# Pooled attention and a softplus feed-forward layer: the transposes of q and of the probabilities in the steady part, by the DMA crossbar instead of TensorE

## The chip, the core and the metric

The kernel runs on one core of a Trainium2 chip. The metric is the device time of one execution in microseconds (us). The engines are named as the profile names them: PE (TensorE; PEld is its weight load), DVE (VectorE), ACT (ScalarE), POOL (GpSimd) and SP (SyncE), whose queue (SPq) issues all transfers of this kernel.

## What is computed

Attention with keys and values that are averaged in eights, then a feed-forward layer with a softplus, all in float32:

```python
# q, k, v: (8, 8, 576, 64)    w_in: (512, 2048)    w_out: (2048, 512)
k_p = k.reshape(B, H, Sp, 8, D).mean(axis=3)            # Sp = 72
v_p = v.reshape(B, H, Sp, 8, D).mean(axis=3)
scores = matmul(q, k_p^T) / sqrt(D)
attn = exp(scores - max) ; attn = attn / (sum(attn) + 1e-9)
x = (attn @ v_p) as rows of 4608 tokens x 512
g = softplus(x @ w_in)
out = g @ w_out                                         # (4608, 512)
```

## The kernel before

The 4608 tokens are worked in 18 chunks of 256 (two tiles of 128). A chunk `c` has its attention, which gives x transposed (512 x 256, split into a high part and a rest, `x` and its low half), and then eight pairs `u` = 0 to 7 of feed-forward blocks. For each pair PE makes the first products `h` (24 matmuls, L687), ACT and DVE turn them into softplus values and their sums (`g`, `gh`, `gl`, `sf`, `so`: L695 to L768), and PE makes the second products `m` (21 matmuls, L839) one pair later. So PE's row in the steady part reads h of pair u, m of pair u-1, h of pair u+1, m of pair u, and so on. In the text below h(7) is the first product of the last pair of a chunk, m(6) the second product of pair 6. ACT's and DVE's work on a pair must be done by the time PE comes to its m.

The attention of the next chunk is fitted in between. In the steady part (`steady_attention` and `probabilities`, chunks 4 to 17) its steps are: SP loads q (256 KB a tile, L363); PE transposes q of both tiles (`qTp<-ident,q`, 8 transposes of 128 x 128, L394) and ACT copies them to `qT` (L401); PE makes the scores into two PSUM banks and half of a third (`sc`, and `m` with kT as operand; L522); DVE takes minima (`mn`, L544) and writes the differences to `E` (L560); ACT takes the exponential of `E` (L355), after the third step of pair 2 (`EXP, third = 2, {}`); DVE takes sums, reciprocals and the probabilities (`pm`, L454, 128 x 512 a tile; `pe`, L570, the last few columns); PE transposes `pm` of both tiles (`ptp`, 8 transposes, L475) and ACT copies them to `pT` (L482); PE transposes `pe` (`ltp`, L575), ACT and DVE split that (`lt__`, L581, L585); PE makes the products with the values (`avp`, L601 and L608); ACT and DVE write x (L615, L618). The first half of h(0) of the next chunk reads this x.

The order on ACT, DVE, PE and SP is not the order of the code. Each step is entered with `op(engine, cost, fn, after, slots)`: a cost in us, the steps it comes after, and the buffers (`Slot`) that it takes. `Order.run` lays all steps of the steady part out in one list by these costs, and the kernel is issued in that order (`tc.manual_schedule`). Each engine then works its own list in order. A step may be laid out only when its slots are free in this plan. What matters below are these kinds:

```python
kinds = {"h": other[:2], "acc": other[2:4], "bank": other[4:], "ld": LD, "q": "a", "pT": "a", "qT": Q, "lt_": "a",
         "pe": "a", "mn": "ab", "sm": "ab", "E": "a", "kp": "a", "vp": "a", "S": "ab", "x": "b",
```

`other` has six PSUM banks, so there are two of kind `bank`. Scores take both until DVE has read them; `qTp` takes two, `ptp`, `ltp` and kT one each, `avp` both. There is one `E`, one `q`, one `pT`, and two `qT`. The weights `wi` of a pair (2 x 512 KB) are loaded again for every chunk and pair (L867) into one of two places, when PE has done the first products of the pair two before.

Of the kernel before, what the change touches and what calls it, by code (L numbers as in the profile page):

```python
# [9 lines left out]
F32 = mybir.dt.float32  # L10
F32R = mybir.dt.float32r
I32 = mybir.dt.int32
AF = mybir.ActivationFunctionType
ALU = mybir.AluOpType
AX = mybir.AxisListType
# [15 lines left out]
class Order:  # L31
# [14 lines left out]
    def op(self, engine, cost, fn, after=(), slots=(), lag=None, rest=0, first=0, table=None, run=None, home=None):  # L46
        o = Op(engine, cost, fn, after, slots, self.HOP if lag is None else lag, len(self.ops))
        o.rest, o.first, o.table, o.run, o.home = rest, first + self.first, table, run, home
        for x in o.after:
            x.followers.append(o)  # L50
        for x in slots:
            x.users.append(o)
        self.ops.append(o)
        return o
# [54 lines left out]
def pooled_attention_softplus_ffn(  # L109
# [9 lines left out]
    nc = tc.nc  # L119
    nc.scalar.preload_act_table_set("exp_and_others")  # L120
    B, H, S, D = q.shape
    NTOK, DM = out.shape
    DFF = w_in.shape[1]
    P = 128
    POOL = 8
    SP = S // POOL
    KM = 64
    KL = SP - KM
    T = 2
    CT = T * P  # L130
    HP = H // 2
# [14 lines left out]
    one = ctx.enter_context(tc.tile_pool(name="one", bufs=1))  # L146
# [95 lines left out]

    wi32, wo32 = w_in.bitcast(I32), w_out.bitcast(I32)
    NS = 3
# [18 lines left out]
    def k_scaled(b, ps):  # L263

        nc.scalar.activation(out=kT[b % 2], in_=ps[:, 0:HP * SP].rearrange("p (m y) -> p m y", m=HP),
                             func=AF.Copy, scale=SCALE)

    def v_scaled(b, vp):
        nc.scalar.activation(out=vs[b % 2], in_=vp, func=AF.Copy, scale=1.0 / POOL)

# [65 lines left out]
    qt_, x_, e_, pt_, last_ = {}, {}, {}, {}, {}  # L336
# [17 lines left out]
    def exponential(E):  # L354
        nc.scalar.activation(out=E, in_=E, func=AF.Exp, scale=-1.0)  # L355

# [27 lines left out]
    class Tile:  # L384
# [49 lines left out]
        def exp_sum(self, j, ps, tag):  # L434
            if j == 0:
                self.sm = small.tile([P, H], F32, tag="sm" + tag, name="sm")
            for m in range(HP):
                h = 4 * (m // 2) + 2 * j + m % 2
                nc.scalar.activation(out=e_[self.c][:, self.t, h], in_=self.view(ps)[:, m],  # L439
                                     func=AF.Exp, scale=-1.0, bias=self.mn[:, j, m:m + 1],  # L440
                                     accum_out=self.sm[:, h:h + 1])
# [60 lines left out]

    order_dep = mybir.DependencyInfo(mybir.DependencyClass.Sync, mybir.DependencyReason.DATA)
    between_out = small.tile([P, 8], F32, tag="between", name="between")
# [367 lines left out]
    op = todo.op  # L875
    ACT, DVE, PE, SYNC = (nc.scalar.engine, nc.vector.engine, nc.tensor.engine, nc.sync.engine)
    todo.begin, todo.table = {SYNC: 0.8}, "exp"

    def bank(s, name):
        if s.tile is None:  # L880
            s.tile = psum.tile([P, 512], F32, tag=s.name, name=name)
        return s.tile
# [3 lines left out]
    def act(n):  # L886
        return 0.14 + 0.00094 * n

    def dve1(n):
        return 0.14 + 0.00054 * n  # L890
# [7 lines left out]
    def weights(f):  # L898
# [5 lines left out]
        def load(i):  # L904
            def fn():
# [4 lines left out]
                else:  # L910
                    st = x["raw", i] = one.tile([P, 4 * 2 * P], I32, tag=stages[i].name, name="wst")
                if i:
# [24 lines left out]
        def bits(k):  # L937
# [4 lines left out]
            else:  # L942
                g = x["g", k] = one.tile([P, 1, 4 * P], I32, tag=gslot[k].name, name="wg")
                up = x["raw", k].unsqueeze(1).rearrange("p x (n w) -> p x n w", w=2)[:, :, :, 1]
# [160 lines left out]
    qT_done, score_done, av_done, k_ready, v_ready, made = {}, {}, {}, {}, {}, {}  # L1105
# [173 lines left out]
    o = op(DVE, 0.3, lambda: x_w.append(ones()), first=2000)  # L1279
# [49 lines left out]
    op = todo.op  # L1329
    EXP, third = 2, {}  # L1330
    HURRY, EARLY = 60, 100
    MM = 0.1142
    x_slot, x_done = {N1: taken[-1]}, {N1: []}
    for x in (qT_done, score_done, av_done, k_ready, v_ready):
        x.clear()
# [4 lines left out]
    def steady_attention(c):  # L1340
        s_q, s_E, s_lt = Slot("q"), Slot("E"), Slot("lt_")
        tiles = [Tile(c, t) for t in range(T)]

        def load():
            load_q(c)
        o_q = op(SYNC, 3.0, load, qT_done.get(c - 1, ()), [s_q], lag=2.4)
        subs = []
        qT_done[c], score_done[c], av_done[c], x_done[c] = [], [], [], []
        sp, s_mn, x_q = spans(c * CT, (c + 1) * CT), Slot("mn"), []
        s_qT, s_qb = [Slot("qT") for _ in tiles], [Slot("bank") for _ in tiles]  # L1350

        def transposes():
            for x, s in zip(tiles, s_qb):
                x.qT(bank(s, "qTp"))
        o = op(PE, 0.89, transposes, [o_q, *av_done.get(c - 1, ())], [s_q, *s_qb], first=EARLY, home="m")
        qT_done[c].append(o)
        for x, s, n in zip(tiles, s_qb, s_qT):
            x_q.append(op(ACT, act(512), lambda x=x, s=s, n=n: x.qT_out(s.tile, n.name), [o], [s, n]))
        old = c - 2 if c - 2 >= NF else None
        ss = [Slot("bank"), Slot("bank"), Slot("acc") if old is None else banks_of[old][3]]  # L1360

        def third_bank():
            return bank(ss[2], "sc") if old is None else ms[old]["rest"]
        p = op(PE, 1.4, lambda: pair_scores(
            c, tiles, [*(bank(s, "sc") for s in ss[:2]), (third_bank(), old is None)]),
               [*x_q, *parts_of(sp, k_ready), m_begun.get(old)], [*s_qT, *ss], first=EARLY, home="m")
        score_done[c].append(p)
        for j in (2, 0, 1):
            ps = lambda j=j: third_bank() if j == 2 else ss[j].tile
            o = op(DVE, 0.3 if j == 2 else 0.68,  # L1370
                   lambda j=j, ps=ps: pair_least(c, j, ps(), s_mn.name), [p], [ss[j], s_mn],
                   first=HURRY if j == 2 else 0)
            for part in range(1 if j == 2 else 3):
                subs.append(op(DVE, 0.3 if j == 2 else (0.46, 0.3, 0.22)[part],
                               lambda j=j, ps=ps, part=part: pair_less(c, j, part, ps()), [o],
                               [ss[j], s_mn, s_E], first=HURRY if j == 2 else 0))
        return lambda where: probabilities(c, tiles, s_E, s_lt, subs, where)

    def probabilities(c, tiles, s_E, s_lt, subs, where):

        s_pT, lows, s_pe, es = Slot("pT"), [], Slot("pe"), []
        ex = op(ACT, 1.2 + TABLE, lambda: exponential(e_[c]), [*subs, where], [s_E])
        op(ACT, TABLE, lambda: None, [ex], first=5000)
        for x in tiles:
            s_sm, s_pm = Slot("sm"), Slot("G")
            o = op(DVE, 0.76, lambda x=x, n=s_sm: x.sum(n.name), [ex], [s_E, s_sm])
            o = op(DVE, 0.38, x.reciprocal, [o], [s_sm])
            m = op(DVE, 0.7, lambda x=x, s=s_pm: x.main(s.name), [o], [s_E, s_sm, s_pm])
            es.append(op(DVE, 0.23, lambda x=x, s=s_pe: pair_ends(c, x, s.name), [o], [s_E, s_sm, s_pe]))
            s = Slot("bank")  # L1390
            o = op(PE, 0.45, lambda x=x, s=s: x.PT(bank(s, "ptp")), [m], [s, s_pm], first=EARLY, home="h")
            lows.append(op(ACT, act(512), lambda x=x, s=s: x.PT_out(s.tile), [o], [s, s_pT]))
        s_l = Slot("bank")
        p = op(PE, 0.23, lambda: pair_last(c, bank(s_l, "ltp")), es, [s_l, s_pe], first=EARLY, home="m")
        for a in range(2):
            h = op(ACT, act(256), lambda a=a: pair_high(c, a, s_l.tile, a), [p], [s_l, s_lt])
            lows.append(op(DVE, dve2(256), lambda a=a: pair_low_ends(c, a, s_l.tile), [h], [s_l, s_lt]))
        for a in range(2):
            lows.append(op(ACT, act(256), lambda a=a: pair_high(c, a, s_l.tile, 2), [p], [s_l, s_lt]))

        def values(after=()):
            sp = spans(c * CT, (c + 1) * CT)
            ss = [Slot("bank"), Slot("bank")]
            o = op(PE, 1.7 if len(sp) == 1 else 2.15,
                   lambda: av_products(c, [bank(s, "avp") for s in ss]),
                   [*lows, *parts_of(sp, v_ready), *after], [*ss, s_lt, s_pT], first=EARLY, home="h")
            av_done[c].append(o)
            return o, ss
        o, ss = values()
        s_x = x_slot[c] = Slot("x")  # L1410
        for r, s in enumerate(ss):
            o = op(ACT, act(512), lambda r=r, s=s: av_high(c, r, s.tile, s_x.name), [o], [s, s_x])
            x_done[c].append(op(DVE, dve2(512), lambda r=r, s=s: av_low(c, r, s.tile), [o], [s, s_x]))
# [171 lines left out]
```

## Time and profile before

| | |
|---|---|
| median of 3 runs | 880.64 us (880.38 to 880.72) |
| span of the profiled execution | 880.5 us |
| PE busy | 869.2 us |
| DVE busy | 644.7 us |
| ACT busy | 418.7 us |
| DMA, HBM traffic over the span | 216 GB/s |

The span reaches from the first to the last instruction of the profiled execution; 0.1 us more lies between it and the median. The steady part repeats every 46.4 us (first products of pair 1 of two neighbouring chunks start at 701.29 and 747.69). In the profile's rows, "x8" counts instructions, the second number of a timeline row is the length of the merged group, and in brackets stands how long the engine sat idle before it and who ended that. A matmul's row includes its way through the array, so neighbouring PE rows overlap: what one costs PE is the distance between starts.

### The profile page before, as it was taken

The numbers are of one execution on the slowest core, as the hardware profiler recorded it, in microseconds if no ns is written. First come the engines' busy times: TensorE is split into PE (matmuls) and PEld (weight loads), VectorE is DVE, ScalarE is ACT, GpSimd is POOL, SyncE is SP. The second block draws the span as 40 slices with busy tenths as digits, with TensorE's granted clock in tenths as the row PEclk, the third lists the DMA queues.
The fourth block names the chain that finished last, engine by engine and source line by source line (L and its number), as shares of the span: only waits on it lengthen the run. The fifth ranks groups of instructions, "written<-read, shape, count | busy, mean of one in ns | idle before, by whom it ended". The sixth has DMA issues, their size and how long they took to land.

```text
span 880.5 us, 21346 instructions
## 1 busy us (share of the span) xinstructions
PE 869.2 (99%) x8706; PEld 845.9 (96%) x8706; DVE 644.7 (73%) x1601; ACT 418.7 (48%) x852; POOL 3.8 (0%) x33
## 2 busy tenths in 40 slices
PE   7999999999999999999999999999999999999997
PEld 5799999999999999999999999999999999999997
DVE  5899999878876868687767766778576565747454
ACT  4964343454454544544454445353545354454432
POOL 1000000000000000000000000000000000000000
PEclk9999999999999999999999999999999999999999
DMA  7975645545888578578757675777566565546472
GB/s 227 323 240 165 216 145 173 169 157 178 292 295 251 216 242 274 188 264 252 243 200 256 228 240 192 240 244 244 196 212 219 182 218 201 216 168 224 165 249 82
DMA packets 107089, 191.17 MB, mean 217 GB/s; under 512 B 46064, under 2 KB 60400, under 8 KB 106992
## 3 DMA queue, kind: packets, MB, share of 16 engines
q1 hardware_dynamic: 106992, 189.82, 64.2%
q8 instruction: 68, 1.11, 0.5%
q14 instruction: 29, 0.24, 0.1%
HBM read 167.25 MB, written 22.54 MB: 216 GB/s over the span
## 4 chain that ended last, share of the span: by engine, by line
PE 96%; DVE 1%; DMA 1%; ACT 1%; issue 0%; SPq 0%; DVEq 0%; ACTq 0%
PE h L687 37%; PE m L839 30%; PE acc L659 7%; PE h L634 7%; PE acc L730 2%; PE avp L601 2%; PE qTp L394 2%; PE ptp L475 2%; PE sc L522 2%; PE avp L608 1%; DMA kvst<-in_k_dram 1%; DMA kvl<-in_v_dram 1%; PE kps L1078 0%; ACT E L439 0%; PE m L522 0%; PE ltp L575 0%
## 5 line engine op out<-in xcount | busy, mean ns | idle before, releaser
L687 PE MATMUL h<-x,l 128*128 128x256 f32 x2748 | 334.9, 278 | 0.0
L687 PEld LDWEIGHTS h<-x,l 128*128 128x128 f32 x2748 | 320.9, 188 | 1.0
L695 ACT ACTIVATE g<-h 128x512 f32<-128x512 f32 x120 | 71.9, 599 | 263.4 <-PE h L687 263.2
L839 PE MATMUL m<-w,so 128*128 128x256 f32 x1134 | 147.1, 276 | 0.0
L839 PEld LDWEIGHTS m<-w,so 128*128 128x128 f32 x1134 | 137.1, 188 | 0.1
L749 DVE TENSOR_TENSOR sf<-g 128x128 f32<-128x128 f32 x112 | 32.7, 292 | 134.6 <-ACT g L695 134.6
L763 ACT CAST so<-sf 128x512 fp32r<-128x512 f32 x112 | 69.7, 622 | 69.1 <-DVE sf L752 68.1
L839 PE MATMUL m<-w,gh 128*128 128x256 f32 x476 | 91.2, 280 | 0.0
L768 DVE TENSOR_TENSOR so<-sf,so 128x512 fp32r<-128x512 f32 x112 | 77.3, 690 | 18.5 <-ACT so L763 16.9
L839 PEld LDWEIGHTS m<-w,gh 128*128 128x128 f32 x476 | 71.8, 188 | 0.0
L716 DVE TENSOR_TENSOR gl<-g,gh 128x384 fp32r<-128x384 f32 (+1 forms) x120 | 67.3, 561 | 3.2 <-ACT gh L709 3.2
L839 PE MATMUL m<-w,gl 128*128 128x256 f32 x238 | 65.8, 277 | 0.0
L709 ACT ACTIVATE gh<-h 128x384 fp32r<-128x384 f32 (+1 forms) x120 | 59.2, 493 | 0.0
L639 ACT ACTIVATE g<-h 128x256 fp32r<-128x256 f32 x96 | 32.1, 383 | 56.0 <-PE h L634 32.7
L634 PE MATMUL h<-x,w 128*128 128x256 f32 x396 | 49.7, 278 | 0.2 <-ACT g L639 0.2
L634 PEld LDWEIGHTS h<-x,w 128*128 128x128 f32 x396 | 47.0, 188 | 0.6 <-ACT g L639 0.3
L659 PE MATMUL acc<-w,g 128*128 128x256 f32 x264 | 46.9, 278 | 0.0
L839 PEld LDWEIGHTS m<-w,gl 128*128 128x128 f32 x238 | 44.7, 188 | 0.0
L860 DVE TENSOR_TENSOR o<-o,m 128x256 f32<-128x256 f32 x98 | 39.7, 418 | 3.3 <-ACT o L852 0.4
L659 PEld LDWEIGHTS acc<-w,g 128*128 128x128 f32 x264 | 39.7, 188 | 0.1
L659 PE MATMUL acc<-w,gl 128*128 128x256 f32 x132 | 36.6, 277 | 0.5 <-DVE gl L645 0.5
L839 PE MATMUL m<-l,gh 128*128 128x256 f32 x196 | 37.0, 277 | 0.0
(216 smaller groups left out, 1323.6 us busy)
## 6 DMA issues: line engine op xcount, KB each, us to landing
l<-wi SPq DMA_DIRECT2D x224, 512.0 KB
out_dram<-o SPq DMA_DIRECT2D x36, 256.0 KB
q<-in_q_dram SPq DMA_DIRECT2D x32, 256.0 KB
kst<-in_k_dram SPq DMA_DIRECT2D x24, 288.0 KB
vst<-in_v_dram SPq DMA_DIRECT2D x24, 256.0 KB
stage<-in_moe_w_in_dram SPq DMA_DIRECT2D x22, 256.0 KB
stage<-in_moe_w_out_dram SPq DMA_DIRECT2D x11, 512.0 KB
wi<-w SPq DMA_DIRECT2D x11, 512.0 KB
```

What stands on the lines that cost most here:

```text
L634: nc.tensor.matmul(out=ps[:, 0:CT], lhsT=row(w, kc), rhs=x[:, kc], start=first and kc == j == 0, stop=last and kc == KC - 1 and j == 2)
L639: nc.scalar.activation(out=g, in_=ps[:, 0:CT], func=AF.Softplus)
L659: nc.tensor.matmul(out=accs[c][t][:, ns], lhsT=a[:, ts], rhs=w[:, ns], start=f == 0 and n == j == 0, stop=f == FC - 1 and n == 1 and j == ...
L687: nc.tensor.matmul(out=ps[:, k * CT:(k + 1) * CT], lhsT=row(w, kc), rhs=x_[c][i][:, kc], start=first and n == 0, stop=last and n == len(or ...
L695: nc.scalar.activation(out=g, in_=x.rearrange("p (b i) -> p b i", i=P), func=AF.Softplus)
L709: nc.scalar.activation(out=gh, in_=quarters(c, x.rearrange("p (b i) -> p b i", i=P)), func=AF.Softplus)
L716: nc.vector.tensor_tensor(out=gl, in0=quarters(c, g), in1=gh.bitcast(F32), op=ALU.subtract)
L749: tt(out=sf[:, 2], in0=g[:, 0], in1=g[:, 2], op=ALU.add)
L763: nc.scalar.copy(out=so[:, 0], in_=ss[c, u])
L768: nc.vector.tensor_tensor(out=so[:, 1], in0=sf, in1=so[:, 0].bitcast(F32), op=ALU.subtract)
L839: nc.tensor.matmul(out=ms[c][n], lhsT=x, rhs=y, start=u == 0 and j == 0 and n in (1, 6, 5, 4), stop=u == FP - 1 and j == 2 and n in (2, 7, ...
L860: nc.vector.tensor_tensor(out=o, in0=in0, in1=m[n], op=how)
```

## The change

The steady part (chunks 4 to 17) transposes q and `pm` by DMA. A 32-bit word is taken apart into two planes of its low and its high 16 bits, each plane is transposed by the crossbar in blocks of 128 x 128, and the planes are joined again. For q: ACT copies each tile into planes (1024 elements of 16 bits a partition), SP issues one transpose a tile (256 KB), which writes back over the q buffer, and DVE joins the planes into `qT`. For the probabilities: DVE copies each tile's `pm` into planes, SP issues one transpose for both tiles (512 KB), which writes a tile `turned` in the place of `E`, and ACT joins each tile's planes into `pT`. The planner has two new numbers, `TURN, TURNED = 1.8, 3.5`, its costs of issuing and of landing.

```diff
+    def split_q(c, t, tag):
+        planes = one.tile([P, 2, DM], U16, tag=tag, name="planes")
+        nc.scalar.copy(out=planes, in_=halves(qt_[c][:, t].rearrange("p h d -> p (h d)")))
+    def turn_q(c, t, planes):
+        nc.sync.dma_start_transpose(out=turned_q(c, t).rearrange("p (j i) -> p j i", i=P),
+                                    in_=planes.rearrange("p w c -> p (w c)"))
+    def merge_q(c, x, tag):
+        nc.vector.tensor_copy(out=halves(x.q.rearrange("p m i -> p (m i)")),
+                              in_=turned_q(c, x.t).rearrange("p (w c) -> p w c", w=2))
+    def split_p(c, x):
+        nc.vector.tensor_copy(out=planes_[c][:, x.t], in_=halves(x.pm.rearrange("p h j -> p (h j)")))
+    def turn_p(c):
+        turned_[c] = one.tile([P, T, 2, HP, P], U16, tag="E", name="turned")
+        nc.sync.dma_start_transpose(out=turned_[c].rearrange("p t w m i -> p (t w m) i"),
+                                    in_=planes_[c].rearrange("p t w c -> p (t w c)"))
+    def merge_p(c, x):
+        nc.scalar.copy(out=pt_[c].bitcast(U16)[:, :, x.t * 2 * P:(x.t + 1) * 2 * P].rearrange(
+            "p m (i w) -> p w m i", w=2), in_=turned_[c][:, x.t])
...
-        o = op(PE, 0.89, transposes, [o_q, *av_done.get(c - 1, ())], [s_q, *s_qb], first=EARLY, home="m")
-            x_q.append(op(ACT, act(512), lambda x=x, s=s, n=n: x.qT_out(s.tile, n.name), [o], [s, n]))
+            o = op(ACT, act(1024), split, [o_q], [s_q, n])
+            o = op(SYNC, TURN, lambda x=x, at=at: turn_q(c, x.t, at["planes"]), [o], [s_q, n],
+                   lag=TURNED)
+            o = op(DVE, dve1(1024), lambda x=x, n=n: merge_q(c, x, n.name), [o], [s_q, n])
...
-            s = Slot("bank")
-            o = op(PE, 0.45, lambda x=x, s=s: x.PT(bank(s, "ptp")), [m], [s, s_pm], first=EARLY, home="h")
-            lows.append(op(ACT, act(512), lambda x=x, s=s: x.PT_out(s.tile), [o], [s, s_pT]))
+            splits.append(op(DVE, dve1(1024), lambda x=x: split_p(c, x), [m], [s_pm, s_pT]))
+        o = op(SYNC, 2 * TURN, lambda: turn_p(c), [*splits, *es], [s_E, s_pT], lag=TURNED)
+        for x in tiles:
+            lows.append(op(ACT, act(1024), lambda x=x: merge_p(c, x), [o], [s_E, s_pT]))
```

`E` is thus held until ACT has joined the planes (`s_E` in the last lines). Before, it was free once `pm` and `pe` were made. The line numbers of the changed kernel are 40 higher in the steps and 45 in the planner's part.

With the new steps the planner lays the whole steady part out anew. Three places show it. The first is PE at the end of a chunk, where the attention of the next one is finished. Before, from the transposes of the last columns (`ltp`) on; the `h` is h(6), and the `m` rows are m(5), whose late weights are `l`:

```order
L575 MATMUL ltp<-ident,pe 64x128 x2
L687 MATMUL h<-x,l 128x256 x24
L601 MATMUL avp<-pT,vs_101 64x256 x8
L608 MATMUL avp<-lt__9873,vlo_103 128x256 x4
L839 MATMUL m<-w,gh 128x256 x2
```

Now, at the same place of the program; the `m` above is m(6), the `h` below is h(0) of the next chunk:

```order
L879 MATMUL m<-l,gl 128x256
L615 MATMUL ltp<-ident,pe 64x128 x2
L641 MATMUL avp<-pT,vs_101 64x256 x8
L648 MATMUL avp<-lt__9946,vlo_103 128x256 x4
L727 MATMUL h<-x,l 128x256 x24
```

Before, h(6) stood between `ltp` and `avp`, and m(5), h(7), m(6) and the transposes of q between `avp` and h(0). Now `ltp`, `avp` and h(0) follow each other with nothing between them. This is so in ten of the fourteen chunks (7 to 16); in the others `ltp` stands earlier and `avp` directly ahead of h(0).

The second place is DVE, where `E` is written. Before, in pair 1, each difference came right behind its minimum, and the exponential followed in pair 2:

```order
L544 TENSOR_REDUCE mn<-m 128x2
L560 TENSOR_TENSOR E<-m,mn 128x2x72
L544 TENSOR_REDUCE mn<-sc 128x7
L749 TENSOR_TENSOR sf<-g 128x128
L750 TENSOR_TENSOR sf<-g 128x128
```

Now the minima still stand in pair 1, and the differences at the end of pair 7, between that pair's `so` and the halves of `ltp` of the chunk that is being finished:

```order
L808 TENSOR_TENSOR so<-sf,so 128x512
L600 TENSOR_TENSOR E<-m,mn 128x2x72
L600 TENSOR_TENSOR E<-sc,mn 128x2x144 x2
L600 TENSOR_TENSOR E<-sc,mn 128x144 x2
L600 TENSOR_TENSOR E<-sc,mn 128x72 x2
L625 TENSOR_TENSOR lt__9946<-ltp,lt__9946 32x256 x2
L658 TENSOR_TENSOR x<-avp,x 128x2x256 x2
```

The scores in question belong to the chunk after the one that is being finished: they are made one chunk ahead and stay in their two banks from pair 2 to the end of pair 7. In the built program the first of these rows waits for ACT's second `pT` copy, `ltp` for the last difference but one, and the second `avp` for the last copy of `lt__`.

The third place is SP's queue around the transpose of the probabilities. `wi_144` and `wi_145` are the weights of pair 7, `wi_130` to `wi_133` those of pairs 0 and 1 of the next chunk. Now:

```order
L907 DMA l<-wi_144 128x1024
L907 DMA l<-wi_145 128x1024
L537 DMA_TRANSPOSE turned<-planes 128x16x128
L907 DMA l<-wi_130 128x1024
L907 DMA l<-wi_131 128x1024
```

Before, the loads followed each other there without it. The two transposes of q stand in the same way ahead of the weights of pairs 4 and 5.

More of the change, by code (lines that the diff above doesn't have):

```diff
@@ L12 @@
 I32 = mybir.dt.int32
+U16 = mybir.dt.uint16
 AF = mybir.ActivationFunctionType
@@ L501, in last_low, with halves, turned_q @@
                 in1=o.bitcast(F32), op=ALU.subtract)
+    def halves(x):
+        return x.bitcast(U16).rearrange("p (c w) -> p w c", w=2)
+    def split_q(c, t, tag):
+        planes = one.tile([P, 2, DM], U16, tag=tag, name="planes")
+        nc.scalar.copy(out=planes, in_=halves(qt_[c][:, t].rearrange("p h d -> p (h d)")))
+        return planes
+    def turned_q(c, t):
+        return qt_[c][:, t].rearrange("p h d -> p (h d)").bitcast(U16)
+    def turn_q(c, t, planes):
+        nc.sync.dma_start_transpose(out=turned_q(c, t).rearrange("p (j i) -> p j i", i=P),
+                                    in_=planes.rearrange("p w c -> p (w c)"))
+    def merge_q(c, x, tag):
+        x.q = one.tile([P, HP, P], F32, tag=tag, name="qT")
+        nc.vector.tensor_copy(out=halves(x.q.rearrange("p m i -> p (m i)")),
+                              in_=turned_q(c, x.t).rearrange("p (w c) -> p w c", w=2))
+    planes_, turned_ = {}, {}
+    def split_p(c, x):
+        if c not in planes_:
+            planes_[c] = one.tile([P, T, 2, H * KM], U16, tag="Z", name="planes")
+        nc.vector.tensor_copy(out=planes_[c][:, x.t], in_=halves(x.pm.rearrange("p h j -> p (h j)")))
[4 more added lines that the diff above has]
+    def merge_p(c, x):
+        if c not in pt_:
+            pt_[c] = one.tile([P, HP, CT], F32, tag="Z", name="pT")
+        nc.scalar.copy(out=pt_[c].bitcast(U16)[:, :, x.t * 2 * P:(x.t + 1) * 2 * P].rearrange(
+            "p m (i w) -> p w m i", w=2), in_=turned_[c][:, x.t])
     order_dep = mybir.DependencyInfo(mybir.DependencyClass.Sync, mybir.DependencyReason.DATA)
@@ L1332, in pooled_attention_softplus_ffn @@
     MM = 0.1142
+    TURN, TURNED = 1.8, 3.5
     x_slot, x_done = {N1: taken[-1]}, {N1: []}
@@ L1349, in steady_attention, with split @@
         sp, s_mn, x_q = spans(c * CT, (c + 1) * CT), Slot("mn"), []
[L1350 to L1354, printed above, removed]
-        o = op(PE, 0.89, transposes, [o_q, *av_done.get(c - 1, ())], [s_q, *s_qb], first=EARLY, home="m")
-        qT_done[c].append(o)
-        for x, s, n in zip(tiles, s_qb, s_qT):
-            x_q.append(op(ACT, act(512), lambda x=x, s=s, n=n: x.qT_out(s.tile, n.name), [o], [s, n]))
+        s_qT = [Slot("qT") for _ in tiles]
+        for x, n in zip(tiles, s_qT):
+            at = {}
+            def split(x=x, n=n, at=at):
+                at["planes"] = split_q(c, x.t, n.name)
+            o = op(ACT, act(1024), split, [o_q], [s_q, n])
+            o = op(SYNC, TURN, lambda x=x, at=at: turn_q(c, x.t, at["planes"]), [o], [s_q, n],
+                   lag=TURNED)
+            o = op(DVE, dve1(1024), lambda x=x, n=n: merge_q(c, x, n.name), [o], [s_q, n])
+            qT_done[c].append(o)
+            x_q.append(o)
         old = c - 2 if c - 2 >= NF else None
@@ L1379, in probabilities @@
     def probabilities(c, tiles, s_E, s_lt, subs, where):
-        s_pT, lows, s_pe, es = Slot("pT"), [], Slot("pe"), []
+        s_pT, lows, s_pe, es, splits = Slot("pT"), [], Slot("pe"), [], []
         ex = op(ACT, 1.2 + TABLE, lambda: exponential(e_[c]), [*subs, where], [s_E])
```

## The prediction

> **What bounds the kernel now.** The page comes first: its busy times, and the shares of the chain of waits that ended last.
>
> ```profile
> span 880.5 us, 21346 instructions
> PE 869.2 (99%) x8706; PEld 845.9 (96%) x8706; DVE 644.7 (73%) x1601; ACT 418.7 (48%) x852; POOL 3.8 (0%) x33
> PE 96%; DVE 1%; DMA 1%; ACT 1%; issue 0%; SPq 0%; DVEq 0%; ACTq 0%
> ```
>
> PE is the bound from end to end. What leaves PE's list is gained, and what makes PE wait is lost, microsecond for microsecond; both are under 0.2% (1.8 us, about what a measurement of this kernel can tell from no change) only if they nearly cancel. The view of who waited for whom, for PE, has as its longest row a start-up wait for q:
>
> ```profile
> PE qTp L394 <- DMA q<-in_q_dram: 1.6, 1, 1.6
> ```
>
> None of its twelve rows lies in the steady part. PE's timeline around a chunk's end shows what is removed, and how the row is built there:
>
> ```profile
> 724.54 1.03 PE L475 MATMUL ptp<-ident,pm 128*128 128x128 f32 x8
> 725.33 0.48 PE L839 MATMUL m<-w,gh 128*128 128x256 f32 x2
> 727.81 0.38 PE L575 MATMUL ltp<-ident,pe 128*64 128x128 f32 x2
> 727.94 2.98 PE L687 MATMUL h<-x,l 128*128 128x256 f32 x24
> 730.86 1.11 PE L601 MATMUL avp<-pT,vs 64*64 64x192 f32 x32
> 732.81 0.48 PE L839 MATMUL m<-w,gh 128*128 128x256 f32 x2
> 735.30 2.88 PE L687 MATMUL h<-x,l 128*128 128x256 f32 x24
> 738.02 0.39 PE L839 MATMUL m<-l,gh 128*128 128x256 f32 x2
> 740.40 1.04 PE L394 MATMUL qTp<-ident,q 128*128 128x128 f32 x8
> 741.19 2.98 PE L687 MATMUL h<-x,l 128*128 128x256 f32 x24
> ```
>
> **What goes.** From start to start, eight transposes of the probabilities take 725.33 - 724.54 = 0.79 us of PE, eight of q 741.19 - 740.40 = 0.79. Fourteen chunks: 14 x 1.58 = 22.1 us off the path. PE pays 0.1 us a block of 128 x 128. The Trainium skill (VectorE: DVE Perf Modes, The three transpose paths) has TensorE at 390 ns a block and the crossbar at 1309, and its rules there send such a block to TensorE where PSUM will do; that speaks against the change. The trace's 0.1 us is the price here, and what the page makes of the DMA is a rival below. By the page's 390 ns the 224 blocks would be 87 us instead of 22, and the sum at the end 882 instead of 947.
>
> **What ACT, DVE and SP get.** ACT's copies that go have the first of these rows. The next three are the nearest for 1024 elements; behind them stand SP's plain transfers and a wait of DVE:
>
> ```profile
> L482 ACT COPY pT<-ptp 128x512 f32<-128x512 f32 x36 | 20.7, 597 | 1.9 <-PE ptp L475 1.7
> L972 ACT CAST w<-stage 128x1024 fp32r<-128x1024 f32 x11 | 11.6, 1058 | 6.4 <-DVE stage L967 6.3
> L956 DVE TENSOR_SCALAR stage<-stage 128x1024 int32<-128x1024 int32 x11 | 7.6, 691 | 0.2
> L967 DVE SCALAR_TENSOR_TENSOR stage<-stage 128x1024 int32<-128x1024 int32 x11 | 13.4, 1223 | 0.2
> L867 SPq DMA_DIRECT2D l<-wi x224: 319/341/1600, 221.6 to 860.7; - x112
> L363 SPq DMA_DIRECT2D q<-in_q_dram x40: 368/574/2052, 3.3 to 741.9; - x40
> 714.37 1.41 DVE L445 TENSOR_REDUCE sm<-E 128x8 f32<-128x576 f32 x2 [1.79 <-ACT E L355]
> ```
>
> ACT gets four copies of 1.06 us a chunk for four of about 0.6, DVE four of 0.69 to 1.22 us (I take the upper, as these copies are strided), 4.9 us of a chunk of over 40 (eight pairs of 5.1 us, below). Neither becomes the bound. q's first joining stands between pair 2's `so` and the sums `sm`, where DVE waits 1.79 us for the exponential anyway. It waits for its transpose, with the sums and pair 3 behind it; if that landed late, DVE would stall by what exceeds those 1.79 us less the copy. q's second joining comes two pairs later. SP's transposes wait for ACT's splits and for DVE's `pe`; the weights behind them are needed two pairs, 10.2 us, later. POOL's step in the scores is not moved.
>
> **Where PE will wait.** PE's list now has `ltp`, `avp`, h(0) in a row, and each of the three hangs on the one before through ACT or DVE. I lay the chain out from the end of h(7), which is 738.02 above, with the rows of ACT and DVE there and of the same steps elsewhere in the chunk:
>
> ```profile
> 719.70 0.60 ACT L695 ACTIVATE g<-h 128x512 f32<-128x512 f32 x1 [1.68 <-PE h L687]
> 724.80 0.60 ACT L695 ACTIVATE g<-h 128x512 f32<-128x512 f32 x1 [2.74 <-PE h L687]
> 730.29 0.36 ACT L581 CAST lt__10509<-ltp 32x256 fp32r<-32x256 f32 x1 [0.48 <-DVE lt__10509 L585]
> 738.71 0.49 ACT L709 ACTIVATE gh<-h 128x384 fp32r<-128x384 f32 x1
> 740.25 0.62 ACT L763 CAST so<-sf 128x512 fp32r<-128x512 f32 x1 [1.05 <-DVE sf L752]
> 703.67 0.31 DVE L560 TENSOR_TENSOR E<-m,mn 128x144 f32<-128x144 f32 x1
> 707.63 1.52 DVE L560 TENSOR_TENSOR E<-sc,mn 128x288 f32<-128x288 f32 x6
> 739.58 0.29 DVE L752 TENSOR_TENSOR sf<-g,sf 128x128 f32<-128x128 f32 x1
> L615 ACT CAST x<-avp 128x512 fp32r<-128x512 f32 x36 | 19.5, 590 | 3.9 <-PE avp L608 3.9
> ```
>
> ACT ends `gh` at 739.20, 1.18 after h(7). Then stand the first joining (1.06, to 2.24), `so` (its `sf` is ready at 1.85; 0.62, to 2.86) and the second joining (to 3.92). Only now is `E` free, and DVE writes the seven differences, 0.31 + 1.52 = 1.83 us; `ltp` waits for the sixth, so it starts at about 5.65. PE ended m(6) at 740.40, that is 2.38: **first wait 3.3 us**. From the start of `ltp` to the end of the last `lt__` copy it is 730.65 - 727.81 = 2.84 us, an alternation of ACT and DVE that h(6) hid before. Now `avp` needs the bank of `ltp` and waits for that copy; `ltp` itself is 0.13 us of PE: **second wait 2.7 us**. After `avp`, h(0) waits for ACT's first copy of x, 0.59 us: **third wait 0.6 us** (before, h(7) and m(6) lay there). Together 6.6 us, in ten chunks 66 us. The ends: 5.4 if both joinings go at 0.6 us as 512 elements do now, 7.6 with 0.25 us more for each of four hops between engines, of which the 0.38 from the end of `sf` (739.87) to `so` (740.25) is the longest in these rows.
>
> The other four chunks lay `avp` directly ahead of h(0), which is 0.6 each, and two of them `avp` behind the next chunk's scores, which hold both banks until their minima and differences are done. I put some 4 us and 2.4 us to these two from the same rows, 8 us for all four, between 5 and 11.
>
> **The clock.** PE's last matmul of the program, two stretches behind it, and the first matmuls:
>
> ```profile
> 875.54 0.28 PE L839 MATMUL m<-l,gl 128*128 128x256 f32 x1
> 877.00:878.00 1.00, 0.00 (x0) 0.00 (x0) 0.40 (x1) 0.00 (x0) 0.00 (x0) 1.00 0.52 203
> 878.00:879.00 1.00, 0.00 (x0) 0.00 (x0) 0.00 (x0) 0.00 (x0) 0.00 (x0) 0.60 0.83 320
> 1.51 3.18 PE L347 MATMUL warm<-ones 128*128 128x512 f32 x4 [1.51 <-DVE ones L342]
> 4.53 1.05 PE L352 MATMUL kps<-ident 128*128 128x128 f32 x8
> L347 PE MATMUL warm<-ones 128*128 128x512 f32 x2 | 2.1, 1142 | 1.5 <-DVE ones L342 1.5
> L1035 PE MATMUL kvlp<-kvl,zl 128*72 128x512 f32 x4 | 2.1, 600 | 0.5 <-DMA kvl<-in_v_dram 0.5
> ```
>
> The column ahead of the DMA share is the granted clock: 1.00 until 878, a mean of 0.60 in the next microsecond, so it halves at 878.2, 2.4 us after PE fell idle at 875.8. Waits of 3.3 and 2.7 us with 0.13 us between them are longer than that. How long the half clock lasts is seen at the start: 512 columns take 1142 ns in the first matmuls and 600 in later ones, while the eight blocks from 4.53 on go in 1.05 us, as q's did above. So full speed came within 3 us of the first matmul at 1.51. I take 3 us at half speed, a loss of 1.5 us a chunk, 15 us in ten, between 0 and 30 (twice as long). The Trainium skill says of this (TensorE: Matmul & The Clock Gate, Why this matters for your kernels) that gaps of over about 3 us bring the half clock back; by that rule the first wait alone would do it, and the trace's 2.4 us agree.
>
> **How long a transpose takes** no row of before shows. The probabilities' one is issued behind the weights of pair 7, which wait for h(5). Pairs are 724.80 - 719.70 = 5.1 us apart, so that is 10.2 us ahead of the end of h(7), less two issues of 0.34; the split of the second tile is done at about the same time. It is needed at 1.18: **cover 10.7 us**. Below: plain transfers of 256-byte pieces, which q's loads are,
>
> ```profile
> 372.00:373.00 1.00, 1.00 (x11) 1.00 (x11) 0.00 (x0) 0.00 (x0) 0.00 (x0) 1.00 1.02 225
> ```
>
> move 225 GB/s with all engines busy, so 512 KB take 2.3 us and 1 MB of weights ahead of them up to 4.7, 7 us in all. Above: pieces of an eighth of that size at the same time a piece, 18.6 us, some 21 with a part of the weights. I take the lower, as the cover holds more than half as much again; each microsecond over the cover would come on top of the chain, in about twelve chunks.
>
> **The sum**, against the profiled execution's 880.5 us: 880.5 - 22.1 + 66 + 8 + 15 = 947.4; the median lies 0.1 above the span, so **947.5 us**.
>
> **Rivals.**
>
> *Without the clock.* If a wait split by `ltp` does not halve it, 880.6 - 22.1 + 74 = 932.5. For it speaks only that the trace has no such gap within the program.
>
> *A slow transpose.* At 21 us the cover is over by 10.3 us, and ACT, waiting at the first joining, holds `so` of pair 7 too: 947.5 + 12 x 10.3 = 1071. It decides from 10.7 us on; at 14.7 us it gives 995. The nearest measured rate speaks against it. By the Trainium skill's page on VectorE named above, 16 blocks one after the other would be 16 x 1.309 = 20.9 us, an estimate; nothing in this trace shows a crossbar transpose.
>
> *All under cover.* The saving stays and nothing waits: 880.6 - 22.1 = 858.5, faster. That needs the differences to be written by the time PE reaches `ltp`, at 2.38 us, where the joinings alone end at 3.92; faster than before it is as soon as the waits of ten chunks come to less than (22.1 - 8) / 10 = 1.4 us each. For it speaks that ACT is 48% busy, against it that its list is worked in order.
>
> *Not by the crossbar at all*, as single 2-byte elements: by the time a piece of the q loads some 300 us a transpose, several times the whole kernel. The program has transposes of whole blocks, so this stays at 1%.
>
> **How the numbers follow.** The forecast 0.71, without the clock 0.11, a slow transpose 0.13, all under cover 0.04, the last 0.01. The low end takes the short chain (54), 5 and no clock: 880.6 - 22.1 + 59 = 917.5. The high end takes 76, 11 and 30, which is 975, and a transpose of 12.4 us, 1.7 over the cover in twelve chunks, 20 more: 995. It leaves out the slow transpose and the fast case, 0.18. Faster 0.04, within 0.2% 0.01, slower 0.95.
>
> **What would show it.** Right: the view of PE's waits has `ltp` (for DVE's `E`) at about 3 us ten times, `avp` (for ACT's `lt__`) at about 2.7 ten times, and h (for ACT's x) at 0.6; DVE's first `E` row waits for ACT's `pT`; the granted clock falls below 1 once a chunk; ACT's first `pT` does not wait for a transfer. Wrong: ACT's `pT` or DVE's `qT` waits for a transfer (a slow transpose), or PE's steady part shows no waits. If the ten waits are there and the clock stays 1.00, the clock's term alone is wrong.

## The result and the profile after

| | before | after |
|---|---|---|
| median | 880.68 us (880.38 to 881.43, 4 runs) | 987.16 us (984.22 to 988.61, 4 runs) |
| ratio | | 1.120, 95% interval 1.118 to 1.122 |
| span of the profiled execution | 880.5 us | 986.2 us |

The changed kernel is 12% slower. The predicted time was 947.5 us, the range 917.5 to 995: the result lies in the range, 40 us above the forecast. The page of the changed kernel, with PE's row, the granted clock in 40 slices, and the chain of waits by engine:

```profile
span 986.2 us, 21092 instructions
PE 904.4 (92%) x8482; PEld 864.8 (88%) x8482; DVE 681.4 (69%) x1657; ACT 451.9 (46%) x852; POOL 3.8 (0%) x33
PEclk9999999997999999897979799897979798998999
PE 83%; ACT 8%; DVE 6%; issue 1%; SPq 1%; DMA 1%; DVEq 0%; ACTq 0%
```

Before, PE was busy for 869.2 of 880.5 us, idle for 11.3. Now it is idle for 81.8 and, although 224 transposes are gone from its list, busy for 35.2 us longer. The clock row, all 9 before, dips about once a chunk. Who waited for whom on PE:

```profile
PE ltp L615 <- DVE E L600: 32.7, 10, 3.3
PE avp L641 <- DVE E L600: 10.3, 2, 6.5
PE avp L641 <- ACT pT L543: 3.3, 2, 1.6
PE h L727 <- ACT x L655: 2.6, 9, 0.4
PE m L562 <- DVE qT L525: 2.5, 1, 2.5
...
PE avp L641 <- ACT lt__7969 L621: 2.1, 1, 2.1
```

Ten such `lt__` rows, one in each of the chunks 7 to 16, come to 18.4 us. One chunk's end on PE:

```profile
606.81 0.87 PE L879 MATMUL m<-w,so 128*128 128x256 f32 x6
...
608.46 0.28 PE L879 MATMUL m<-l,gl 128*128 128x256 f32 x1
611.95 0.64 PE L615 MATMUL ltp<-ident,pe 128*64 128x128 f32 x2 [3.20 <-DVE E L600]
612.51 0.47 PE L641 MATMUL avp<-pT,vs 64*64 64x64 f32 x2
615.09 1.98 PE L641 MATMUL avp<-pT,vs 64*64 64x64 f32 x30 [2.10 <-ACT lt__7969 L621]
617.00 2.02 PE L648 MATMUL avp<-lt__7969,vlo 96*128 96x64 f32 x8
618.84 4.40 PE L727 MATMUL h<-x,l 128*128 128x256 f32 x24
```

PE ends m(6) at 608.74, waits 3.2 us for the differences, then 2.1 us for the copies of `ltp`. The 24 matmuls of h(0) take 4.40 us where the pairs of the chunks around it take 2.88 to 3.09. ACT and DVE over the same time:

```profile
606.80 0.49 ACT L749 ACTIVATE gh<-h 128x384 fp32r<-128x384 f32 x1
607.17 1.38 ACT L543 COPY pT<-turned 128x1024 uint16<-128x1024 uint16 x1
608.39 0.64 ACT L803 CAST so<-sf 128x512 fp32r<-128x512 f32 x1
608.90 1.35 ACT L543 COPY pT<-turned 128x1024 uint16<-128x1024 uint16 x1
```

```profile
582.87 0.75 DVE L525 COPY qT<-q 128x1024 uint16<-128x1024 uint16 x1
...
610.28 0.31 DVE L600 TENSOR_TENSOR E<-m,mn 128x144 f32<-128x144 f32 x1 [0.54 <-ACT pT L543]
610.51 1.52 DVE L600 TENSOR_TENSOR E<-sc,mn 128x288 f32<-128x288 f32 x6
```

ACT comes from `gh` straight to the first joining, with no wait for the transfer; DVE's differences wait for the second (DVE's first row is a joining of q). The clock there (column ahead of the DMA share):

```profile
610.00:611.00 1.00, 0.00 (x0) 0.00 (x0) 0.71 (x3) 0.25 (x1) 0.00 (x0) 1.00 1.22 275
611.00:612.00 1.00, 0.06 (x1) 0.06 (x2) 1.00 (x5) 0.00 (x0) 0.00 (x0) 0.76 1.04 235
612.00:613.00 1.00, 0.99 (x4) 0.41 (x4) 0.03 (x1) 0.37 (x2) 0.00 (x0) 0.50 0.00 1
...
620.00:621.00 1.00, 1.00 (x7) 1.00 (x6) 0.97 (x3) 0.00 (x0) 0.00 (x0) 0.50 0.00 0
621.00:622.00 1.00, 1.00 (x7) 1.00 (x7) 0.86 (x3) 0.00 (x0) 0.00 (x0) 0.62 0.00 0
```

A mean of 0.76 in the microsecond from 611 means that it halved at 611.5, 0.62 that it came back at 621.8: half speed (a granted clock of 0.50) for 10.2 us. Added up over all such rows of one microsecond, busy share times the missing part of the clock, half speed cost 51.9 us of PE's work in the program: 40.7 in the ten chunks 7 to 16, about 4.1 in each, and 11.2 in four stretches ahead of them. So the 105.7 us are: 22.1 less for the transposes, 70.5 more idle, 51.9 of half clock, and 5.4 that this sum leaves over.

### The profile page after: what moved, and what is told of

Same layout as the page of the kernel before. It is cut to its first block, busy times and chain, and to the rows that moved or that the text cites. A ratio compares the mean times of both kernels' runs of the same rounds, so it can differ in the third digit from the quotient of the medians.

```text
span 986.2 us, 21092 instructions
## 1 busy us (share of the span) xinstructions
PE 904.4 (92%) x8482; PEld 864.8 (88%) x8482; DVE 681.4 (69%) x1657; ACT 451.9 (46%) x852; POOL 3.8 (0%) x33
## 4 chain that ended last, share of the span: by engine, by line
PE 83%; ACT 8%; DVE 6%; issue 1%; SPq 1%; DMA 1%; DVEq 0%; ACTq 0%
PE h L727 36%; PE m L879 24%; PE acc L699 7%; PE h L674 7%; PE avp L641 3%; ACT pT L543 3%; DVE E L600 2%; PE acc L770 2%; PE avp L648 2%; PE sc L562 1%; ACT g L735 1%; ACT so L803 1%; DMA stage<-in_moe_w_out_dram 1%; PE ltp L615 1%; ACT gh L749 1%
## 5 line engine op out<-in xcount | busy, mean ns | idle before, releaser
L727 PE MATMUL h<-x,l 128*128 128x256 f32 x2748 | 358.5, 289 | 2.6 <-ACT x L655 2.6
L727 PEld LDWEIGHTS h<-x,l 128*128 128x128 f32 x2748 | 344.9, 200 | 6.0 <-ACT x L655 5.1
L641 PE MATMUL avp<-pT,vs 64*64 64x256 f32 (+3 forms) x384 | 37.9, 461 | 32.1 <-DVE E L600 10.3
L641 PEld LDWEIGHTS avp<-pT,vs 64*64 64x64 f32 x384 | 19.1, 186 | 45.3 <-issue 11.5
L679 ACT ACTIVATE g<-h 128x256 fp32r<-128x256 f32 x96 | 32.1, 382 | 55.6 <-PE h L674 32.7
L658 DVE TENSOR_TENSOR x<-avp,x 128x512 fp32r<-128x512 f32 x36 | 23.8, 687 | 42.6 <-ACT x L655 42.5
```

Of the source, the lines that this page charges most:

```text
L641: nc.tensor.matmul(out=ps[e * D:(e + 1) * D, g * CT + t.start:g * CT + t.stop], lhsT=vs[i][rows, n], rhs=pt[rows, n, t], start=g == 0 and ...
L727: nc.tensor.matmul(out=ps[:, k * CT:(k + 1) * CT], lhsT=row(w, kc), rhs=x_[c][i][:, kc], start=first and n == 0, stop=last and n == len(or ...
```

## The experiments

The theory: the dropped wait of the scores for avp lets them run one chunk ahead; they hold both banks until `E` is free, `E` now holds the turned probabilities until ACT has joined them, and so `ltp` waits at the chunk's end; the half clock follows from these waits. The rivals: the crossbar is slow, the longer copies cost, or the chain of one chunk has become longer than the chunk. Ratios are against the kernel before, timed beside each run, with 95% intervals.

| run | median us | ratio | clock |
|---|---|---|---|
| scores wait for avp again | 910.0 | 1.033 (1.029 to 1.036) | 0.980 |
| own buffers for `turned` | 915.3 | 1.039 (1.037 to 1.040) | 0.979 |
| waits filled, too much | 986.2 | 1.121 (1.117 to 1.125) | 0.986 |
| only the probabilities | 924.9 | 1.050 (1.049 to 1.052) | 0.988 |
| waits filled, half | 954.3 | 1.083 (1.082 to 1.085) | 0.987 |
| both edits | 908.3 | 1.033 (1.030 to 1.036) | 0.982 |
| both, other figure in the plan | 912.0 | 1.035 (1.032 to 1.037) | 0.987 |
| only q | 880.9 | 0.999 (0.998 to 1.001) | 0.998 |
| both, landing told to the plan | 882.6 | 1.002 (1.001 to 1.004) | 0.990 |
| and the first chunk's on PE | 886.4 | 1.006 (1.004 to 1.007) | 0.993 |
| and kT out of the way | 882.0 | 1.001 (0.999 to 1.002) | 0.985 |

The clock is the mean granted one of each run's profiled execution. All rows are read from that execution, which need not lie at the median: with both edits and the other figure in the plan the executions spread from 902.3 to 920.2 us, and the profiled one is the fastest.

**The order put back.**

```diff
-               [*x_q, *parts_of(sp, k_ready), m_begun.get(old)], [*s_qT, *ss], first=EARLY, home="m")
+               [*x_q, *parts_of(sp, k_ready), m_begun.get(old), *av_done.get(c - 1, ())],
+               [*s_qT, *ss], first=EARLY, home="m")
```

> The changed kernel with one thing put back: the scores of chunk c + 1 wait again for the products avp of chunk c, as q's transposes on TensorE did before. All crossbar transposes and all copies stay. Theory (the wait comes from scores that run one chunk ahead and hold both PSUM banks while E is held by the turned probabilities; the half clock follows from the wait): PE waits for E at ltp in none of the chunks; avp waits for ACT's second joining, which by the rows of the changed kernel ends about 4.5 us after h(7) where m(6) ends at 2.5, so about 2.0 us, and h(0) 0.6 us for x; no gap over 2.4 us, so the granted clock stays at 1.00 in the steady part. 858.5 + 12 x 2.6 = about 890 us, between 870 and 905. Rival (the crossbar's transposes and the longer copies themselves are what is paid): they are all still there, so over 960 us.

910.0 us; the waits of `ltp` for `E` are gone. PE's longest waits:

```profile
PE avp L641 <- ACT pT L543: 22.7, 13, 4.8
PE h L727 <- ACT x L655: 4.3, 12, 0.4
```

So 77 of the 106 us hang on one dependency, with every transpose and copy still there: the first two rivals fall as the main cause. The time is 5 us over the expected range's end, and the clock did not stay at 1.00 as expected: eight stretches of half speed cost 15.5 us. Most follow only the wait for `pT` of 1.4 to 1.65 us and that for x of 0.25 to 0.45, as here:

```profile
381.04 1.36 PE L641 MATMUL avp<-pT,vs 64*64 64x256 f32 x16 [1.40 <-ACT pT L543]
383.52 4.21 PE L727 MATMUL h<-x,l 128*128 128x256 f32 x24 [0.25 <-ACT x L655]
```

In other chunks of this run the same waits left h(0) at 2.99 to 3.10.

**Own buffers.** The turned probabilities get buffers other than `E`'s; with that their one transpose becomes two, one a tile.

```diff
-        turned_[c] = one.tile([P, T, 2, HP, P], U16, tag="E", name="turned")
+        turned_[c, t] = one.tile([P, 2, HP, P], U16, tag=tag, name="turned")   # tag of a Slot("G"), one a tile
```

> The changed kernel, but the turned probabilities go into two buffers of their own kind (the tags of g), one transpose for each tile, instead of into the buffer of E. Scores still run one chunk ahead. Theory: E is free as soon as the sums, pm and pe are done, so the differences of the next chunk are written a pair earlier and the banks are free when PE reaches ltp; the wait of ltp for E goes and with it the half clock. PE then waits for pT and x at most: 865 to 900 us. If running ahead alone (two banks held for longer) is what costs, E's buffer makes no difference and it stays over 960. Rival (slow transposes or copies): two transposes for one make it no faster, over 960.

915.3 us, 15 over the expected range's end (half speed cost 15.7 us), also without the ten waits of `ltp`. Either edit alone takes them away: scores that run ahead cost them only because `E` is not free, and `E` only because the scores run ahead. What stands in their place is new, in the view of ACT's waits:

```profile
ACT pT L543 <- DMA turned<-planes: 38.7, 14, 5.5
```

**Filled waits.** Products of the identity, used by nothing, in the ten chunks, first 28 ahead of `ltp` and 14 behind it:

```diff
+            fill(c, 28)
             pair_last(c, bank(s_l, "ltp"))
+            fill(c, 14)
```

> The changed kernel with transposes of the identity into an unused PSUM bank put into PE's two waits of the ten chunks: 28 of about 0.1 us ahead of ltp, 14 behind it. They compute nothing that is used. The waits on E and on the lt copies stay as they are, only PE is not idle in them. Theory: the granted clock stays at 1.00 in these ten chunks, and what half speed costs there goes: from the windows of the changed kernel's trace about 4.1 us a chunk, so 987 - 41 = about 946 us, between 938 and 955. Rival (the stretched matmuls are only an effect of waiting, or the fills lengthen the chain): no change, 980 to 995.

986.2 us, no change. Each product is two instructions, 0.11 us apart (56 in 6.4 us; the row below has their least, middle and greatest length in ns):

```profile
L353 PE MATMUL fill<-ident x840: 270/275/377, 386.1 to 888.7; 128*128 128x128 f32 x168
```

840 for 420 products: the fills lasted 6.4 and 3.4 us and put off what the clock gave back. That run decides nothing; with 13 and 6:

> As the run with filled waits, with 13 and 6 products of the identity in place of 28 and 14: each product turned out to be two instructions, so the first fills lasted 6.4 and 3.4 us where PE waited 3.2 and 2.1, and lengthened the chain by about 4 us a chunk, as much as the clock gave back. These should last 3.0 and 1.45 us. They compute nothing that is used. Theory (half speed is what the changed kernel pays beside the waits): the granted clock stays at 1.00 in the ten chunks and the time is about 987 - 41 = 946 us, between 938 and 958. Rival (the clock's loss is hidden by the chain behind the waits): 975 to 990 again.

954.3 us. The ten waits of `ltp` have shrunk to

```profile
PE ltp L615 <- DVE E L600: 4.0, 10, 0.4
```

and half speed costs 9.3 us instead of 51.9, none of it in these chunks. The time fell by 33 us with PE's chain of waits left as long as it was. So the clock is a loss of its own. Of the 42.6 us that the clock gave back the span kept 34.6; where the other 8 went is open.

**Only the probabilities.** q's lines are those of the kernel before.

> Only the probabilities go by the crossbar; q is transposed by TensorE as in the kernel before, with the wait for avp that this operation carried. Theory: the scores come after avp again, so ltp does not wait for E, and the clock stays at 1.00; 11 us of the transposes are gone (0.79 x 14), and avp waits about 2.0 us for ACT's second joining and h(0) 0.6 us for x in about twelve chunks: 880.6 - 11 + 31 = about 900 us, between 875 and 912. Rival (the probabilities' transpose, four times q's in one DMA, and its joinings are the cost): nearly all of the loss stays, over 950 us.

924.9 us, 13 over the range. `ltp` does not wait, and PE's longest wait is the one expected, for the second joining, 1.6 us a chunk:

```profile
PE avp L641 <- ACT pT L543: 20.7, 13, 1.7
PE m L879 <- DVE E L600: 4.8, 11, 0.9
PE h L727 <- ACT x L655: 4.7, 12, 0.4
```

By the profiled execution (921.9) PE is idle for 32.5 us more than before, as laid out (31); the sum missed 10.0 us of half clock, and about 10 more lie in PE's rows without either.

**Only q.** The probabilities' lines are those of the kernel before.

> Only q goes by the crossbar, without the wait for avp; the probabilities are transposed by TensorE as in the kernel before. The planner then lays the scores two pairs behind avp by itself, since the transposes need the banks. Theory (no bank is held early, E is free early): 880.6 - 11 = about 870 us, between 866 and 882, with the clock at 1.00. Rival (q's transposes, DVE's joining ahead of the sums, or SP's list cost): over 890 us.

880.9 us: no difference, where 11 us less were expected. The executions spread from 877.0 to 883.6, and the profiled one is the fastest of twelve, at a clock of 0.998; the others have 0.993 to 0.998. In it PE is idle for 14.7 us, 3.4 more than before, 2.5 of them in one wait for q's joining. The rest of the loss lies in executions without a profile; their lower clock is what can be seen of it.

**Both edits.**

> Both edits together: the scores wait for avp again, and the turned probabilities have two buffers and a transpose each. All crossbar transposes and copies stay. Theory: E and the banks are free early, the joinings of the two tiles stand two pairs apart on ACT, where ACT waits for PE anyway, and PE waits only for x in the chunks that lay avp directly ahead of h(0): 858.5 + about 10 = 868 us, between 860 and 885. If the transposes' landing or the copies cost by themselves, it stays near the two single edits, 900 or more.

> As the run with both edits, with the planner's figure for what a transpose takes of SP's list 1.3 us instead of 1.8, so that it lays avp behind an h and ahead of an m in ten of thirteen chunks, as in the kernel before, instead of in six. Theory: h(0) waits for x in fewer chunks, 862 us, between 857 and 875. If a tile's transpose lands later than 4.8 us after its issue, ACT waits for it at pT and it is slower than the run before it, up to 890.

908.3 and 912.0 us, not 868 and 862, and no better than the order alone (910.0). The second run tells the plan that a tile's transpose takes 1.3 us of SP's list instead of 1.8 (`TURN = 1.3`). The theory was incomplete: with the waits for `E` gone the next thing in line is the transfer. In the second run SP issues the first tile's transpose, and ACT comes to its joining:

```profile
599.36 1.24 SPq L537 DMA_TRANSPOSE turned<-planes  x1
```

```profile
608.11 1.37 ACT L543 COPY pT<-turned 128x1024 uint16<-128x1024 uint16 x1 [3.17 <-DMA turned<-planes]
```

8.75 us from issue to landing. In the first run all fourteen chunks have this wait, 43.7 us of ACT, and the transposes landed 7.7 to 11.2 us after their issue; the plan reckons with 5.3 (1.8 + 3.5), in the second with 4.8.

**The transpose by itself.** Eight transposes behind the end of the program, each with a copy by ACT behind it:

```diff
+        for blocks in (16, 8, 4, 1, 16, 8, 4, 1):
+            n = blocks * P
+            nc.sync.dma_start_transpose(out=flat(seen)[:, 0:n].rearrange("p (b i) -> p b i", i=P),
+                                        in_=flat(alone)[:, 0:n])
+            nc.scalar.copy(out=flat(alone)[:, 0:n], in_=flat(seen)[:, 0:n])
```

> The changed kernel with eight more crossbar transposes behind its last output, one after the other with a copy by ACT between them, of 16, 8, 4 and 1 blocks of 128 x 128 and the same again; they move zeros and nothing uses them. No weights move beside them. Theory (the 8.5 us from issue to landing in the steady part is mostly the weights ahead of them in the same queues): 16 blocks, the probabilities of a chunk, land in about 3 to 5 us, and 8 blocks in 2 to 4. Rival (the crossbar itself takes that long, by the page's 1.3 us a block): 16 blocks in about 21 us, 8 in 10.5, 1 in 1.3 and a fixed part.

ACT's rows of the second round; the bracket is the time from the copy before to the landing:

```profile
1002.96 1.90 ACT L1613 COPY alone<-seen 128x2048 uint16<-128x2048 uint16 x1 [3.75 <-DMA seen<-alone]
1007.67 1.04 ACT L1613 COPY alone<-seen 128x1024 uint16<-128x1024 uint16 x1 [2.82 <-DMA seen<-alone]
1011.20 0.62 ACT L1613 COPY alone<-seen 128x512 uint16<-128x512 uint16 x1 [2.48 <-DMA seen<-alone]
1014.19 0.30 ACT L1613 COPY alone<-seen 128x128 uint16<-128x128 uint16 x1 [2.38 <-DMA seen<-alone]
```

16 blocks land in 3.75 us, one in 2.38: (3.75 - 2.38) / 15 = 0.09 us a block and 2.3 fixed. So of the 8.75 us of 8 blocks in the steady part 2.8 are the transpose, and the rest is there only where weights move beside it. That it is waiting behind them in the queues fits, but was not tried apart.

**The landing told to the plan.**

```diff
-    TURN, TURNED = 1.8, 3.5
+    TURN, TURNED = 1.25, 7.5
+    # and first=60 for the splits, transposes and joinings of the probabilities
```

> The run with both edits (scores wait for avp; the turned probabilities in two buffers of their own), with the planner told what the runs measured: 1.25 us of SP's list for a tile's transpose and 7.5 us more until it has landed (before: 1.8 and 3.5), and with the splits, transposes and joinings of the probabilities put ahead of other work that is ready. In the two runs with both edits ACT stood at its first joining for 2.6 to 4.6 us a chunk until the first tile had landed, some 8.5 us after its issue. Theory (it is not the crossbar's price but where the plan puts the joinings): ACT's waits for the transfer go below 1 us, PE waits only for x in the four chunks that lay avp directly ahead of h(0), and the clock has a few short half-speed stretches: 858.5 + about 10 = 868, between 862 and 880, faster than before. Rival (landing 8.5 us late makes the chain of a chunk longer than a chunk's 46 us whatever the plan): PE still waits about 2 us a chunk at avp, 900 or more.

882.6 us, 2.6 over the expected range's end; ACT waits for a transfer once, for 0.6 us. The plan's figures and the priority of these steps (`first=60`) were changed together, so what each gave is not told apart. Nearly all that is left in the profiled execution is one place, the first of the fourteen chunks, where the joinings stand behind casts of the weights:

```profile
230.78 0.70 PE L641 MATMUL avp<-pT,vs 64*64 64x128 f32 x8 [6.36 <-ACT pT L543]
235.06 1.56 PE L641 MATMUL avp<-pT,vs 64*64 64x128 f32 x24 [3.58 <-ACT pT L543]
```

Two runs tried to mend what remained: the probabilities of that chunk on TensorE, then also kT's steps moved out of avp's way (`first=0` for its transposes, `first=200` for ACT's scaling and for the joinings of the probabilities). Both also put the splits and transposes of the probabilities further ahead (`first=200`) and have `TURNED = 6.5`.

> The run before it (both edits, the planner told the landing) with one more exception: in the first of the fourteen chunks, whose attention runs while the weights are still being combined on ACT and DVE, the probabilities are transposed by TensorE as in the kernel before; landing time told to the planner 1.25 and 6.5 us, splits and transposes of the probabilities put further ahead. In the run before it PE waited in this one chunk for 6.4 and 3.6 us behind joinings that stood behind casts of the weights, and lost 4.9 us to the half clock after them: 14.9 us of its 879.8. Theory: these go, 0.8 us of TensorE comes back, the rest stays: 879.8 - 14.9 + 0.8 = 866, between 862 and 874, faster than the kernel before by over 0.7%. Rival (the waits come back elsewhere, since the chain of a chunk is as long as the chunk): 876 or more.

> The run before it with the keys' transposes kT taken out of avp's way: their operation on PE no longer has a place ahead of others, ACT's scaling of them is put ahead of other ready work, and so are the joinings of the probabilities. In the run before it avp stood behind ACT's kT three times for about 1.3 us with a wait of h for x behind it, and kT stood 4.1 us for its sums. The plan now lays avp behind an h and ahead of an m in twelve of fourteen chunks. Theory (single places in the plan are what is left, not the crossbar): about 878 - 11 = 867 in the profiled run, median between 862 and 876, faster than the kernel before. Rival (each chunk's chain is too long by the transposes' landing, so that a wait mended at one place opens at another): 878 or more.

886.4 and 882.0 us, not 866 and 867: both lie where their rival, that a wait mended at one place opens at another, put them. The waits aimed at are gone, except kT's for its sums, and others have opened. The last run's longest:

```profile
PE kT L260 <- DVE kp L253: 4.2, 2, 3.1
PE m L879 <- DVE gl L756: 3.1, 2, 1.6
PE m L879 <- DVE E L600: 2.3, 4, 1.0
...
PE m L879 <- DVE o L900: 1.4, 2, 1.1
```

Its profiled execution has a span of 883.9: 880.5 - 22.1 + 0.8 for the eight transposes put back, 12.1 more idle than before, 9.8 of half clock in three places, and 2.8 left over. No version that is faster than the kernel before was found; the best are level with it.

## Why the prediction was right, and where not

- **What goes** and what bounds: right. The time rose by what PE waits and by its clock. That it lies within the range is in part luck: the high end of 995 holds 20 us for a transpose that lands 1.7 us over its cover in twelve chunks, and that did not happen. Without it the high end is 975, and the measured 987 lies above, for the clock took more than its own upper end of 30.
- **First wait**, 3.3 us in ten chunks: 32.7 / 10 = 3.27, for `E`, with `ltp` 5.7 us after h(7) where 5.65 was laid out. The chain was the right one, step by step. Putting back the order, or a second buffer, removed it.
- **Second wait**, 2.7: 1.84 on average; in eight of the ten chunks two `avp` matmuls run ahead of it, in the bank that is free. In the chunk shown it is 3.1 us from the start of `ltp` to the rest of avp, 0.3 more than laid out; there `ltp` itself ran at half clock.
- **Third**, 0.6: 0.3, 2.6 us in all. The waits of the ten chunks come to 53.7 us, at the low end of 54 to 76. The other four cost 16 (10.3, 3.3 and 2.5 in the rows above) where 8 were taken with an end at 11. Together, with what the start adds, 70.5 against 74.
- **The clock** is the term that was mis-sized: 15 us in ten chunks with ends of 0 and 30, and 40.7 measured in these ten, 51.9 in all. The step that failed is "I take 3 us at half speed", read off the lengths of the program's first matmuls (the clock column of the profile before stands at 1.00 there). Half speed lasted 10.2 us in each of the ten chunks, in the one shown from 611.5, still in the first wait, until 6.7 us after the second; and PE worked through most of it. Nor does it begin a fixed time after PE falls idle, 2.4 us as laid out: it begins 2.8 to 4.3 us after, in seven of the ten chunks only when the first wait has ended. Its beginnings in these chunks, 393.1, 447.7, 502.3 us and so on to 884.6, lie 54.6 us apart each time, 16 times 3.413, while the first waits begin 53.9 to 56.1 us apart. The Trainium skill (TensorE: Matmul & The Clock Gate, What's actually happening) has the gate decide in free-running windows of 3413 ns; the lengths here, 3.4, 6.8, 10.2 and 13.6 us, agree, and so do these beginnings. Its rule of gaps over about 3 us (Why this matters for your kernels) is too mild for this kernel: the run with the order put back has half-speed stretches behind waits of 1.4 and 0.25 us, 2.2 us apart.
- **The rival without the clock** falls: with the waits filled, 33 us went.
- **Landing of the transposes**: under the cover, as taken. SP's row of the chunk shown above,

```profile
596.36 5.09 SPq L537 DMA_TRANSPOSE turned<-planes  x1
```

and ACT's joining at 607.17 make a cover of 10.8 us against 10.7; over all fourteen chunks it is 7.7 to 11.3. ACT waited for a transfer once, for 0.8 us, where SP issues at 323.60 and the joining starts at 332.00: that transpose took 8.4 us to land, so "I take the lower", 7 us, was 1.4 too low. Of these 7 the transpose itself had 2.3; alone, 16 blocks took 3.75. The Trainium skill's 1309 ns a block (VectorE: DVE Perf Modes, The three transpose paths) is no measure for many blocks in one transfer: 0.09 us each here. Yet this rival decides in the mended kernels, whose plan left a cover of 5.3.
- **Copies**: on ACT the splits take 1.05 us as taken, the joinings 1.35 where 1.06 was taken; on DVE 0.69 and 0.75, the lower end and not the upper. ACT at 46% and DVE at 69% stayed off their bounds. The splits (least, middle and greatest of 28, in ns):

```profile
L513 ACT COPY planes<-q x28: 1040/1046/1048, 190.0 to 795.8; 128x1024 uint16<-128x1024 uint16 x28
...
L533 DVE COPY planes<-pm x28: 680/685/689, 218.9 to 919.4; 128x1024 uint16<-128x1024 uint16 x28
```

- **All under cover**, 858.5: given 0.04, and no run reached it. Of 21 us saved the last run gave back 12 in waits and 10 in half clock.

## What to carry to other kernels

When an operation is replaced, look at the waits it carried for others: here q's transposes carried a dependency and the probabilities' left a buffer free. Putting back either one gave 72 to 77 us, over three times the 22 that the transposes had cost. A step that moves from a short path (0.8 us of PE and 0.6 of ACT) to a transfer of 8 us has to be started 8 us earlier or it comes back as waits, and a planner needs the landing under load (7.7 to 11.2 us here), not alone (2.8). On TensorE a wait of a few microseconds is to be priced with the half clock behind it, which outlasts it: 70.5 us of waits brought 51.9 more here.

## What the runs showed of the hardware

- Two waits of 3.2 and 2.1 us with 1.0 us of work between them bring 10.2 us of half clock. Waits of 1.4 to 1.65 and 0.25 to 0.45 us, about 2 us of avp apart, bring 3.4 us in some chunks and nothing in others of the same run.
- In every trace that has several stretches of half speed, all begin on one grid of 3.41 us. When the traces are cut along it, every piece of 3.41 us at full granted clock with PE busy for a share under 0.48 was followed by half speed, and none with a share over 0.67; between the two both occur, and the runs don't show what decides there. So the longest single wait alone does not decide here.
- A crossbar transpose of 8 blocks holds SP's queue for 1.24 us and one of 16 blocks in the steady part for 4.7 to 6.1 in thirteen chunks and 1.64 in one, but that of 16 at the program's end for 1.6 at most:

```profile
L537 SPq DMA_TRANSPOSE turned<-planes x14: 1642/4952/6059, 221.5 to 921.7; - x14
```

- PE runs 4% slower for some stretches at a granted clock of 1.00: 24 matmuls of h take about 2.99 us instead of 2.88 for seven pairs in a row from 570 to 606 in the changed kernel, up to the waits shown above, and pairs are 5.3 us apart instead of 5.1. The runs don't say why. What is left over in the sums above may lie in such stretches; that was not added up.

```profile
603.28 2.99 PE L727 MATMUL h<-x,l 128*128 128x256 f32 x24
...
637.37 2.88 PE L727 MATMUL h<-x,l 128*128 128x256 f32 x24
```
